# Loads of stage 3, from batch 2 on, issued by ScalarE in place of SyncE, with new due times

## The chip, the cores and the metric

The kernel runs on one core of a Trainium2 chip. The metric is the device time of one execution in microseconds, and the time of a kernel is the median of its runs. Three runs of the kernel before were timed; a fourth execution was profiled, and the rows below come from that one.

## What is computed

The input `x` has 8 batches of 2496 tokens with 256 channels. Each batch is transformed along the tokens with a real FFT, multiplied with a complex filter (one row for each of 1249 frequencies), and transformed back. The 19968 rows that come out go through a layer of 8 experts: the expert of a token is a hash of its id, and each token's row becomes `relu(row @ w1[e]) @ w2[e]` with 1024 hidden values.

```python
X = np.fft.rfft(x, axis=1)
y = np.fft.irfft(X * (filt_r + 1j * filt_i)[None], n=x.shape[1], axis=1).reshape(B * S, D)
expert_idx = token_ids * np.int64(2654435761) % np.int64(E)
for e in range(E):
    mask = expert_idx == e
    out[mask] = np.maximum(y[mask] @ w1[e], 0.0) @ w2[e]
```

## The kernel before, in words

**The filter, batch by batch.** 2496 is 39 times 64, so a transform is made in stages of small matmuls. Stage 1 (`stage1`, L581) multiplies along the 39; its result goes to a scratch tensor `d1` in DRAM (L605) and comes back with rows and columns regrouped (`load2`, L607). Stage 2 is five pieces for each batch: `forward` (L627) takes a piece to the frequencies and multiplies the filter in, `back` (L637) takes it back: TensorE makes eight matmuls, ScalarE copies the two results to SBUF (L644) and issues two DMAs of 256 KB that write them into the scratch tensor `d2` in DRAM (L646). Stage 3 (`stage3`, L662) multiplies along the 39 again; it needs the whole of `d2`, regrouped. `load4` (L648) fetches it in three parts into the tiles `t4`, of which there are two buffers: parts 0 and 1 are one DMA of 960 KB each, part 2 is two DMAs, of 480 and 160 KB. So a batch has four load4 DMAs, and the six batches from batch 2 on have 24. Each part serves two stage 3 pieces. A stage 3 piece is up to eight matmuls (L673), a copy by ScalarE (L676), two sums on VectorE (L677, L678), and four scatters by GpSimd that write each token's row to its place in the tensor `xs`, sorted by expert and stage (L708). Batches 0 and 1 are done ahead of the main loop by other functions that don't use this `load4`.

**The experts, tile by tile.** `xs` is worked off in tiles of 256 tokens, each with one expert. For each tile there is a `step(i)` (L1373); from tile 42 on it is `late_step`, with no filter work. SyncE issues the loads of the tile's two weight matrices, 1 MB each (`weights`, L739 and L742), two tiles ahead, and SyncE or ScalarE those of its rows (`load`, L1155). GpSimd makes sums of weights (`tw`, L1187). `up` (L1191) is the first product: seven products of four matmuls into three PSUM banks. ScalarE copies the first result out (`h21`, L1209). TensorE then makes products b and c, and after those the next product adds into bank a, which that copy has to have read; VectorE needs the copy as well for its sums (L1205); then come ScalarE's relus (L1202). `down` (L1228) is the second product, four blocks of eight matmuls (L1233).

**What sets the order.** Every engine works its instructions off in the order in which the program names them, and a DMA issue is an instruction of the engine that issues it. The filter's pieces are laid between the tiles by hand: `put(b, ...)` gives every piece of batch b a due time, and `run_until(t)` (L1360) emits all pieces due before t. In step i the blocks are: `run_until(i + .03)` ahead of `up`; `run_until(i + .6)` between `up` and `down`; three more inside `down`, at i + .7, .8 and .9; and `run_until(i + 1)` behind `down`, after the load of the second weight matrix. So a piece due at 18.55 is emitted between `up` and `down` of tile 18, and one due at 19.02 ahead of `up` of tile 19.

```python
run_until(i + .03)
...
up(i, ht, lambda: ask(i))
weights(i + 2, 0)
...
run_until(i + .6)
down(i, ht, lambda k: spot(i, k))
weights(i + 2, 1)
run_until(i + 1)
```

The last `back` of a batch is due at 4.48 (batch 2), 10.5, 18.5, 23.5, 31.5 and 36.5 (batch 7), so in the block between `up` and `down` of tiles 4, 10, 18, 23, 31 and 36. Before the change part 0 of load4 stands in the same block, behind it. The first stage 3 piece of each batch is due one to two tiles later (5.75, 11.85, 19.85, 24.85, 33.65, 38.65).

Of the kernel before, what the change touches and what calls it, by code (L numbers as in the profile page):

```python
# [221 lines left out]
def kernel(  # L222
# [10 lines left out]
    nc = tc.nc  # L233
# [99 lines left out]
    class Batch:  # L333
# [183 lines left out]
        def load4(self, v):  # L517
            self.t4[v] = t4pool.tile([NK, XL, C], F32, name=f"t4_{self.b}_{v}", tag="t4")
            for dram, chip in self.parts(self.d2, self.t4[v], v):
                nc.sync.dma_start(out=chip, in_=dram)  # L520
# [25 lines left out]
    class Folded(Batch):  # L546
# [101 lines left out]
        def load4(self, w):  # L648
            self.t4[w] = t4pool.tile([NK, XL, C], F32, name=f"t4_{self.b}_{w}", tag="t4")
            for dram, chip in self.moves(self.d2, self.t4[w], w):  # L650
                nc.sync.dma_start(out=chip, in_=dram)

        def room(self, u):

# [421 lines left out]
    def put(b, **at):  # L1076

        return [(t, lambda u=u, kind=kind: getattr(batches[b], kind)(u)) for kind, ts in at.items()
                for u, t in enumerate(ts) if t is not None]
# [4 lines left out]
    def row(t, n=5):  # L1084
        return [t + k for k in range(n)]
# [2 lines left out]
    todo += [(.76, lambda: [nc.sync.dma_start(out=dram, in_=chip) for dram, chip in put_off[3]])]  # L1088
    todo += [(2.3, places2)]
    todo += put(2, forward=[1.5, 1.62, 2.5, 2.62, 3.5], back=[2.48, 2.49, 3.48, 3.49, 4.48], load2=[None] * 4 + [1.63],  # L1090
                load4=[4.55, 5.1, 6.2], stage3=[5.75, 5.85, 6.65, 6.85, 7.65, 7.85])
    todo += put(3, load1=[None, None, .9], fold=[None, None, 2.8], stage1=[None] * 4 + [3.65, 3.75],
                load2=[4.1, None, 5.5, None, 7.1], forward=row(5.55), back=row(6.5), load4=[10.55, 11.3, 13.9],
                stage3=row(11.85, 6))
    todo += put(4, load1=[4.3, 6.05, 8.3], fold=[5.8, 7.8, 9.8], stage1=row(6.75, 6),
                load2=[12.05, None, 13.5, None, 15.5], forward=row(13.55), back=row(14.5), load4=[18.55, 19.3, 21.9],
                stage3=[19.85, 20.85, 21.85, 22.85, 23.65, 23.85])
    todo += put(5, load1=[10.3, 12.3, 14.1], fold=[11.8, 13.8, 15.8], stage1=[12.75, 13.75, 14.75, 15.75, 16.65, 16.75],
                load2=[17.05, None, 18.5, None, 20.5], forward=row(18.55), back=row(19.5), load4=[23.55, 24.3, 25.9],
                stage3=[24.85, 25.65, 25.85, 26.65, 26.85, 27.65])  # L1100
    todo += put(6, load1=[16.1, 17.3, 20.1], fold=[17.8, 19.8, 21.8], stage1=row(18.75, 6),
                load2=[24.05, None, 25.5, None, 28.5], forward=row(26.55), back=row(27.5), load4=[31.55, 32.3, 34.9],
                stage3=[33.65, 34.65, 35.65, 36.65, 37.65, 37.85])
    todo += put(7, load1=[22.1, 23.3, 26.1], fold=[23.8, 25.8, 27.8], stage1=row(24.75, 6),
                load2=[30.05, None, 31.5, None, 33.5], forward=row(31.55), back=row(32.5), load4=[36.7, 37.9, 39.9],
                stage3=[38.65, 38.85, 39.85, 40.85, 41.85, 42.85])
    for e, ts in enumerate(((27.05, 28, 28, 28, 29, 29.5), (28.1, 29, 29, 30, 30, 31.05), (30.05, 31, 31, 31, 32, 33.05),
                            (31.1, 32, 32, 33, 33, 34.05), (33.1, 34, 34, 34, 35, 36.05), (34.1, 35, 35, 36, 36, 37.05),
# [343 lines left out]
```

## Time and profile before

| what | value |
|---|---|
| median of three runs | 1374.3 us (1368.91 to 1377.05) |
| the profiled execution | 1381.9 us |
| its span, first to last instruction | 1380.1 us |
| mean granted TensorE clock over it | 0.991 |
| TensorE, VectorE, GpSimd, ScalarE busy | 96%, 70%, 60%, 30% of the span |
| step 0 to step 41, with the filter work of batches 2 to 7 | about 152 to 900 us |

PE is TensorE, DVE is VectorE, ACT is ScalarE, POOL is GpSimd, SP is SyncE; PEld are TensorE's weight loads. A "q" behind the name marks what an engine's sequencer does, DMA issues above all: the duration of a DMA row is that of the issue, not of the transfer. `t<-d` is a load4 DMA, `d<-mid` a write of a result into `d1` or `d2`, `mid<-d` a load2, `x<-in_x_dram` a load of input, `wts` a weight matrix, `xg<-xs` a tile's rows. In a timeline row the bracket tells how long the engine had stood idle before, and what ended that.

### The profile page before, as it was taken

Reading aid. Unit: us, or ns where it says so; the run is one execution under the profiler, and the core shown is the slowest. Engines: PE = TensorE matmul, PEld = TensorE weight load, DVE = VectorE, ACT = ScalarE, POOL = GpSimd, SP = SyncE. Lnnn points to the kernel's source line nnn. Section 1 sums busy time; section 2 is a strip of 40 time slices with the busy share of each in tenths; the row PEclk is TensorE's granted clock in tenths of the full one; section 3 lists DMA queues with packets and bytes.
Section 4 is the critical chain, followed back from the end, with each engine's and each line's share of the span. In section 5 each row is a group of like instructions: output and inputs, shape, how many; then the busy total and the mean of one; then the engine's idle time right before and its main releaser. Section 6 shows DMA issues by size and latency. Waiting matters only on the chain.

```text
span 1380.1 us, 34551 instructions
## 1 busy us (share of the span) xinstructions
PE 1329.8 (96%) x13490; PEld 1197.0 (87%) x13490; DVE 962.4 (70%) x1758; ACT 408.2 (30%) x749; POOL 826.1 (60%) x724
## 2 busy tenths in 40 slices
PE   8998999999999999989999998999999999999997
PEld 7776868788888888877888887899999999999997
DVE  6786585775576667747767786677777777777775
ACT  3546213232223222322222222122222222222222
POOL 2156526575566626748858787875665556655563
PEclk9999999999999999999999999999999999999999
DMA  8757787978787789696899878654243523271421
GB/s 229 214 187 247 172 257 190 270 216 240 189 231 234 231 233 287 174 232 198 269 308 243 249 224 241 169 178 133 63 122 102 167 76 107 48 222 41 135 49 36
DMA packets 232640, 255.74 MB, mean 185 GB/s; under 512 B 124363, under 2 KB 200896, under 8 KB 225861
## 3 DMA queue, kind: packets, MB, share of 16 engines
q1 hardware_dynamic: 124116, 163.08, 41.3%
q10 hardware_dynamic: 88357, 45.86, 13.9%
q0 software_dynamic: 20000, 44.53, 9.9%
q8 instruction: 109, 1.79, 0.6%
q14 instruction: 58, 0.48, 0.1%
HBM read 303.04 MB, written 86.15 MB: 282 GB/s over the span
## 4 chain that ended last, share of the span: by engine, by line
PE 81%; DMA 7%; DVE 5%; issue 2%; POOL 2%; ACT 1%; SPq 1%; ACTq 0%; another core or an unknown queue 0%; POOLq 0%; DVEq 0%
PE dps L1233 18%; PE up_b L1198 7%; PE up_a L1198 5%; PE dnb L1256 5%; PE upa L1256 5%; PE dna L1256 5%; PE dnc L1256 5%; PE upc L1256 5%; PE up_c L1198 4%; PE pd L673 3%; PE pa L593 3%; PE upg L1256 2%; PE upb L1256 2%; PE upe L1256 2%; PE dne L1256 2%
## 5 line engine op out<-in xcount | busy, mean ns | idle before, releaser
L1233 PE MATMUL dps<-wts,ht 128*128 128x256 f32 x1344 | 313.4, 384 | 1.1 <-ACT ht L1202 1.1
L1233 PEld LDWEIGHTS dps<-wts,ht 128*128 128x128 f32 x1344 | 252.7, 191 | 64.0 <-ACT ht L1202 24.2
L1330 POOL DMA_INDIRECT out_dram<-osb,nos x158 | 172.2, 1090 | 209.3 <-DVE osb L1271 162.6
L708 POOL DMA_INDIRECT xs<-o,sidx x176 | 181.6, 1032 | 180.0 <-DVE o L677 102.6
L1187 POOL TENSOR_TENSOR tw<-wts 128x512 f32<-128x512 f32 x158 | 203.7, 1289 | 92.8 <-DMA wts<-in_moe_w_dram 66.2
L1187 POOL TENSOR_TENSOR tw<-wts,tw 128x512 f32<-128x512 f32 x158 | 205.5, 1301 | 4.8
L1205 DVE TENSOR_TENSOR ht<-up_b,ht 128x512 f32<-128x512 f32 x126 | 87.1, 691 | 85.3 <-PE up_b L1198 59.0
L1202 ACT ACTIVATE ht<-ht 128x512 f32<-128x512 f32 x126 | 79.4, 630 | 174.3 <-DVE ht L1205 155.3
L1268 ACT ACTIVATE ht<-ht 128x512 f32<-128x512 f32 x114 | 71.7, 631 | 143.2 <-DVE ht L1271 96.4
L1198 PE MATMUL up_a<-xt,wts 128*128 128x128 f32 x672 | 95.7, 275 | 1.1 <-PE warm L1030 0.7
L1198 PEld LDWEIGHTS up_a<-xt,wts 128*128 128x128 f32 x672 | 88.3, 192 | 3.6 <-PE warm L1030 0.9
L1198 PE MATMUL up_b<-st,tw 128*128 128x128 f32 x672 | 89.3, 276 | 2.2 <-DVE ht L1205 1.4
L1205 DVE TENSOR_TENSOR ht<-up_c,ht 128x512 f32<-128x512 f32 x84 | 58.0, 691 | 41.1 <-PE up_c L1198 24.0
L1198 PEld LDWEIGHTS up_b<-st,tw 128*128 128x128 f32 x672 | 81.7, 192 | 3.0 <-issue 2.8
L1256 PE MATMUL dna<-wts,ht 128*64 128x128 f32 (+1 forms) x1152 | 79.5, 273 | 0.0
L1256 PE MATMUL upa<-filt,wts 128*64 128x128 f32 (+1 forms) x1136 | 77.5, 273 | 0.0
L1209 ACT COPY ht<-up_a 128x512 f32<-128x512 f32 x42 | 24.6, 586 | 178.0 <-PE up_a L1198 145.0
L309 DVE TENSOR_TENSOR filt<-ht 128x512 f32<-128x512 f32 x76 | 57.6, 758 | 26.6 <-ACT ht L1268 26.6
L673 PE MATMUL pd<-t,wi_t 120*117 120x256 f32 (+1 forms) x264 | 65.0, 387 | 8.1 <-DMA t<-d 8.0
L1256 PEld LDWEIGHTS dna<-wts,ht 128*64 128x64 f32 (+1 forms) x1152 | 69.4, 140 | 0.3 <-ACT ht L1268 0.2
L593 PE MATMUL pa<-x,wf_t 117*120 117x256 f32 (+1 forms) x264 | 66.1, 394 | 3.1 <-issue 1.7
L1256 PEld LDWEIGHTS upa<-filt,wts 128*64 128x64 f32 (+1 forms) x1136 | 67.6, 139 | 0.1
(231 smaller groups left out, 2541.0 us busy)
## 6 DMA issues: line engine op xcount, KB each, us to landing
wts<-in_moe_w_dram SPq DMA_DIRECT2D x162, 1024.0 KB
d_t<-t2s SPq DMA_DIRECT2D x19, 1024.0 KB
e_t<-t2s SPq DMA_DIRECT2D x19, 1024.0 KB
d<-mid ACTq DMA_DIRECT2D x60, 256.0 KB
mid<-d SPq DMA_DIRECT2D x24, 512.0 KB
x<-in_x_dram SPq DMA_DIRECT2D x39, 312.0 KB
t<-d SPq DMA_DIRECT2D x12, 960.0 KB
d<-mid ACTq DMA_DIRECT2D x11, 960.0 KB
```

The source lines that it names most:

```text
L309: eng.tensor_tensor(out_, a, b, op=op)
L593: nc.tensor.matmul(out=ps[0:cols, i - i0, :], lhsT=wf2_t[:, kind, 0:cols], rhs=self.x[w][:, i if kind == 0 else 2 * n - 1 - i, :], start=T ...
L673: nc.tensor.matmul(out=ps[kind][0:m, i, :], lhsT=wi2_t[0:r, kind, 0:m], rhs=self.t4[w][0:r, place(w, kind, 2 * half + i)[0], :], start=Tru ...
L708: st = nc.gpsimd.indirect_dma_start(out=xs[:], out_offset=bass.IndirectOffsetOnAxis(ap=index, axis=0), in_=rows, in_offset=None, bounds_ch ...
L1187: eng.tensor_tensor(t[k][:], p, q, op=OP.subtract)
L1198: nc.tensor.matmul(out=ps[bank][:, f, :], lhsT=w[:, f * P:(f + 1) * P], rhs=xx, start=first and f == 0, stop=True, skip_group_check=True)
L1202: nc.scalar.activation(out=out, in_=in_, func=AF.Relu)
L1205: nc.vector.tensor_tensor(out, ps[bank][:], other, op=OP.add)
L1233: nc.tensor.matmul(out=ps[:, h, :], lhsT=ht[:, h, fp, :], rhs=w2[:, fp, :], start=(fp == 0), stop=(fp == FP - 1))
L1256: nc.tensor.matmul(out=out[c:c + n], lhsT=w[:, c:c + n], rhs=xx, start=first, stop=True, skip_group_check=True)
L1268: nc.scalar.activation(out=out, in_=in_, func=AF.Relu)
L1330: st = nc.gpsimd.indirect_dma_start(out=out[:], out_offset=bass.IndirectOffsetOnAxis(ap=to_rows[i][:, h:h + 1], axis=0), in_=o[:, h, :], i ...
```

## The change

`load4` issues its DMAs from ScalarE's queue and no longer from SyncE's, and the due times of its parts are changed. Part 0 moves from the block between `up` and `down` to the one ahead of the next tile's `up` (in batch 2 from between to behind `down` of tile 4). Part 1 stays in its block in batches 2 to 6 (there behind the first filter piece of the next batch, where one is due in that block), and moves from behind stage 3's last piece in `down` of tile 37 to ahead of `up` of tile 38 in batch 7. Part 2 stays where it was in batch 2; in batches 3 to 7 it stands in the last block of its tile.

```diff
         def load4(self, w):
             self.t4[w] = t4pool.tile([NK, XL, C], F32, name=f"t4_{self.b}_{w}", tag="t4")
             for dram, chip in self.moves(self.d2, self.t4[w], w):
-                nc.sync.dma_start(out=chip, in_=dram)
+                nc.scalar.dma_start(out=chip, in_=dram)
...
-                load4=[4.55, 5.1, 6.2], stage3=[5.75, 5.85, 6.65, 6.85, 7.65, 7.85])
+                load4=[4.95, 5.1, 6.2], stage3=[5.75, 5.85, 6.65, 6.85, 7.65, 7.85])
...
-                load2=[4.1, None, 5.5, None, 7.1], forward=row(5.55), back=row(6.5), load4=[10.55, 11.3, 13.9],
+                load2=[4.1, None, 5.5, None, 7.1], forward=row(5.55), back=row(6.5), load4=[11.02, 11.55, 13.95],
...
-                load2=[12.05, None, 13.5, None, 15.5], forward=row(13.55), back=row(14.5), load4=[18.55, 19.3, 21.9],
+                load2=[12.05, None, 13.5, None, 15.5], forward=row(13.55), back=row(14.5), load4=[19.02, 19.55, 21.95],
...
-                load2=[17.05, None, 18.5, None, 20.5], forward=row(18.55), back=row(19.5), load4=[23.55, 24.3, 25.9],
+                load2=[17.05, None, 18.5, None, 20.5], forward=row(18.55), back=row(19.5), load4=[24.02, 24.55, 25.95],
...
-                load2=[24.05, None, 25.5, None, 28.5], forward=row(26.55), back=row(27.5), load4=[31.55, 32.3, 34.9],
+                load2=[24.05, None, 25.5, None, 28.5], forward=row(26.55), back=row(27.5), load4=[32.02, 32.55, 34.95],
...
-                load2=[30.05, None, 31.5, None, 33.5], forward=row(31.55), back=row(32.5), load4=[36.7, 37.9, 39.9],
+                load2=[30.05, None, 31.5, None, 33.5], forward=row(31.55), back=row(32.5), load4=[37.02, 38.02, 39.95],
```

## Rows read from the trace of the kernel before

**Rows 1.** The page's first part: busy time of each engine over the span.
```profile
PE 1329.8 (96%) x13490; PEld 1197.0 (87%) x13490; DVE 962.4 (70%) x1758; ACT 408.2 (30%) x749; POOL 826.1 (60%) x724
```

**Rows 2.** The waits: who waited for what, us in total, times, longest.
```profile
PE pd L673 <- DMA t<-d: 8.0, 3, 4.8
```

**Rows 3.** Timeline of PE: start, us, instruction, [idle before <- what ended it].
```profile
250.83 1.99 PE L673 MATMUL pd<-t,wi_t 120*117 120x256 f32 x8 [1.66 <-DMA t<-d]
...
604.17 3.56 PE L673 MATMUL pd<-t,wi_t 120*117 120x256 f32 x8 [4.85 <-DMA t<-d]
...
625.82 1.96 PE L673 MATMUL pd<-t,wi_t 120*117 120x256 f32 x8 [1.47 <-DMA t<-d]
```

**Rows 4.** Three stretches: busy of PE, PEld, DVE, ACT, POOL; PEclk, DMA share, GB/s.
```profile
196.00:200.00 4.00, 3.72 (x15) 2.41 (x16) 3.92 (x7) 0.00 (x0) 1.48 (x1) 0.72 0.94 293
...
600.00:604.00 4.00, 0.00 (x0) 0.00 (x0) 0.00 (x0) 0.00 (x0) 0.00 (x0) 1.00 1.13 228
604.00:608.00 4.00, 3.83 (x10) 2.98 (x11) 0.16 (x1) 0.58 (x1) 0.00 (x0) 0.58 1.07 364
```

**Rows 5.** Timeline of SyncE: load4 issues of batches 2, 3, 5 and 7.
```profile
243.24 0.36 SPq L651 DMA_DIRECT2D t<-d  x1
...
348.11 0.36 SPq L651 DMA_DIRECT2D t<-d  x1
...
581.87 6.13 SPq L561 DMA_DIRECT2D x<-in_x_dram  x3
588.11 0.90 SPq L651 DMA_DIRECT2D t<-d  x1
...
605.55 0.39 SPq L651 DMA_DIRECT2D t<-d  x1
...
860.22 8.32 SPq L651 DMA_DIRECT2D t<-d  x2
```

**Rows 6.** All load4 issues by line: duration in ns, least, median and longest.
```profile
L651 SPq DMA_DIRECT2D t<-d x24: 310/422/2029, 243.2 to 868.2; - x24
```

**Rows 7.** Timeline of ScalarE: last filter writes, next tile's copies, three instructions by them.
```profile
232.50 1.23 ACTq L646 DMA_DIRECT2D d<-mid  x2
...
239.17 0.58 ACT L1209 COPY ht<-up_a 128x512 f32<-128x512 f32 x1 [6.70 <-PE up_a L1198]
...
343.55 1.10 ACTq L646 DMA_DIRECT2D d<-mid  x2
...
349.55 0.58 ACT L1209 COPY ht<-up_a 128x512 f32<-128x512 f32 x1 [2.13 <-PE up_a L1198]
...
525.78 1.07 ACT L596 COPY mid<-pa 120x512 f32<-120x512 f32 x2 [7.58 <-DMA d<-mid]
...
584.04 0.37 ACT L676 COPY o<-pd 78x256 f32<-78x256 f32 x1 [1.74 <-PE pd L673]
...
593.79 0.85 ACTq L1155 DMA_DIRECT2D xg<-xs  x2
...
726.61 1.10 ACTq L646 DMA_DIRECT2D d<-mid  x2
...
734.14 0.58 ACT L1209 COPY ht<-up_a 128x512 f32<-128x512 f32 x1 [7.56 <-PE up_a L1198]
...
807.97 1.23 ACTq L646 DMA_DIRECT2D d<-mid  x2
...
816.36 0.58 ACT L1209 COPY ht<-up_a 128x512 f32<-128x512 f32 x1 [6.35 <-PE up_a L1198]
...
869.31 0.59 ACT L1209 COPY ht<-up_a 128x512 f32<-128x512 f32 x1
```

**Rows 8.** Timeline of PE: three places where its idle time or its order matters.
```profile
196.28 1.09 PE L623 MATMUL pb<-mid,filt 64*64 64x512 f32 x8 [2.20 <-DVE filt L633]
...
240.76 0.61 PE L1198 MATMUL up_a<-xt,wts 128*128 128x128 f32 x4
...
534.01 1.16 PE L1198 MATMUL up_c<-st,wts 128*128 128x128 f32 x8 [1.25 <-DVE ht L1205]
```

## The prediction

> **What bounds the kernel now.** I read the page's busy shares first, then the waits, then the timelines around load4. TensorE is busy for 1329.8 of 1380.1 us [rows 1], so at most some 50 us of its idle time can go at all, and a change to load4 can win only what TensorE waits for load4. The waits view gives that sum: three waits for `t<-d`, 8.0 us [rows 2]. The timeline shows them singly [rows 3]: 1.66 us ahead of batch 2's first stage 3 piece, then 4.85 and 1.47 us ahead of batch 5's first and third. The 4.85 has a second price: eight matmuls that took 1.99 us at 250.83 took 3.56 behind it, and the stretch 604 to 608 shows a granted clock of 0.58 where the one before had 1.00 [rows 3, 4]: for most of it the engine ran at 1.2 GHz in place of 2.4. That is 3.56 - 1.99 = 1.57 us more. All that load4 costs now is therefore 1.66 + 4.85 + 1.57 + 1.47 = 9.55 us. The other 21 DMAs of load4 land in time.
>
> Where the loads wait: SyncE issues them in its own order. Batch 5's part 0 was issued at 588.11, right behind three input loads that held SyncE from 581.87 to 588.00, and part 1 at 605.55 [rows 5]. The writes that part 0 needs had been issued by ScalarE in tile 23's block, one tile before.
>
> **The change, step by step.** The sum is made as differences of the profiled execution (span 1380.1 us, the execution 1381.9) and laid on the median of 1374.3, which is 7.6 us under it; I take no other difference between the two.
>
> *The issues.* 24 issues leave SyncE and come to ScalarE, at a median of 0.42 us each and 2.03 at most [rows 6]: about 10 us of ScalarE, which is busy for 408.2 us of the span [rows 1]. That costs nothing where ScalarE would stand idle, and its idle time before the next copy hides it in most places (1.74 to 7.56 us in the bracketed rows of ScalarE) [rows 7]. Where that cover is gone, as at 869.31, each DMA adds its 0.42 to the next copy.
>
> *Batch 5, parts 0 and 1.* ScalarE comes free at 584.41 (584.04 + 0.37) [rows 7], so part 0 goes out 588.11 - 584.41 = 3.7 us sooner. TensorE's wait ended 16.06 us after the issue (604.17 - 588.11) [rows 3, 5], in a stretch where the DMA engines were full (share 1.13 and 1.07) [rows 4]. If that 16 us stays, the wait shrinks from 4.85 to 1.15 us; after one of 1.66 us the clock held [rows 3], so the 1.57 go too. At best, if the load no longer stands behind the input loads, all 4.85 go; at worst the full engines only deliver in another order and nothing of this wait goes. I take 3.7 + 1.57 = 5.27, as the nearer row is the issue's own. Part 1 goes out ahead of the row loads at 593.79, some 12 us before 605.55 [rows 5, 7], for a wait of 1.47 us: all of it goes. The Trainium skill, DMA: Bandwidth & Descriptors, section "Issuing engines are not separate DMA queues", speaks against more than this: all queues share the same 16 DMA engines, so that another issuing engine saves only the time of issuing. By that rule the sum stays as I take it. The same page, section "Queues, rings and completion order", lets each DMA engine take turns between the queues that have work. By that rule the whole 4.85 would go and the sum would be 1.15 us lower; the trace of before can't decide, since no load4 of it left ScalarE's queue.
>
> *Batch 2, part 0: a new wait ahead of a copy.* The load reads what ScalarE's last two filter writes put into DRAM, so its issue waits until they have landed. In batch 2 they were issued from 232.50 to 233.73, and SyncE could issue the load only at 243.24 [rows 5, 7]. On ScalarE the load now stands ahead of tile 5's copy, which ran at 239.17 [rows 7]. The copy, and behind it the relus of tile 5 and VectorE's sums that need the copy, start at 243.24 + 0.42 = 243.66, so 4.5 us late. TensorE needs the copy's end, 239.75, only at 240.76, when it writes into bank a again [rows 7, 8]: 1.0 us of cover, and TensorE stands for 3.5 us. The 1.66 us at 250.83 vanish behind that, since the load is issued when it was. Does the clock fall? It did after 4.85 us, not after 1.66 us [rows 3, 4]; after 2.20 us at 196.28 the stretch 196 to 200 shows 0.72 [rows 4, 8]. So I charge the 1.57 again. Bounds: no stall, if the writes land as fast as in batch 3 (3.5 us after the issue: 344.65 to 348.11 [rows 5, 7]); 1 to 2 us more if the row loads and weights, which SyncE no longer holds back from 236 to 243, press on the writes. I take 3.5 + 1.57 = 5.07, the row of batch 2 itself. The Trainium skill, Perfetto Trace Analysis, section "DMA Instruction — HWDGE (DVE, Sync)", warns that the confirmation of a write can take surprisingly long where the target is HBM. The trace agrees: 3.5 us in batch 3, 9.5 in batch 2.
>
> *Part 0 of the other batches.* In batch 3 the writes had landed at 348.11; 0.42 more gives 348.5, ahead of the copy at 349.55 [rows 5, 7]: nothing. In batch 6 they were issued by 727.71 and the copy runs at 734.14, in batch 7 by 809.20 and at 816.36 [rows 7]; with the middle of 3.5 and 9.5, 6.5 us, they land at 734.2 and 815.7. I charge 0.5 us for batch 6, nothing for 7; batches 4 and 5 lie like 3 and 7.
>
> *Part 2.* Its two DMAs came back to back, but in batch 7 SyncE took 8.32 us for the pair, so an issue can wait on an older transfer as well [rows 5]. On ScalarE the pair stands ahead of the next tile's copy. At best 0.84 us inside idle time; at worst 8.3 us less the cover. Most pairs went in about the median, so I charge only batch 7, where ScalarE has no idle time ahead of 869.31 [rows 7]: 0.84 less part of the 1.0 us cover, 0.5 us.
>
> *What is freed.* SyncE's queue gives row loads and weights out sooner. TensorE waits for neither in the waits that I found, so this wins nothing; GpSimd's scatters follow stage 3 and keep their order.
>
> *The sum:* -5.27 - 1.47 - 1.66 + 5.07 + 0.5 + 0.5 = -2.3 us, so 1372.
>
> **The rivals.**
> (a) *All late loads come early.* Batch 5's first wait goes whole, and if the 7.58 us for which ScalarE stood at 525.78 hang on part 1 of batch 4, which now goes out a tile's time sooner, the 1.25 us of TensorE at 534.01 go too [rows 7, 8]. Batch 2's stall stays, without the fall of the clock: -9.55 - 1.25 + 3.5 = -7.3, 1367. For it: the input loads do stand ahead of the load. Against: the DMA engines are full where it would have to land sooner.
> (b) *ScalarE stands in the wait for its own writes in batch after batch* (slower). Mechanism: part 0 ahead of the tile's copy, while the writes land. It decides as soon as the writes take longer than the time from their issue to the copy plus 0.6 us: 7 us in batch 6, 7.7 in 7, 5.5 in 3. With batch 2's 9.5 us everywhere, the copies start at 354.57, 737.63 and 819.12, 5.0, 3.5 and 2.8 us late; less 1.0 each, 4.0, 2.5 and 1.8 us, and the clock falls in two of them: 8.3 + 3.1 = 11.4 us, in place of the 0.5 of batch 6. -2.3 + 10.9 = +8.6, 1383. For it: nothing but 10 us of DMA traffic separates batch 2 from the others. Against: batch 3's 3.5 us.
> (c) *The issue moves, the landing doesn't.* Full DMA engines deliver batch 5's load when they did; only 1.47 and 1.66 go, and the costs stay: -3.13 + 6.07 = +2.9, 1377. In batches 2 and 3 the issue can't move at all, since SyncE already issued when the writes landed.
>
> **How the numbers follow.** A measurement of this kernel can tell about 0.5%, 6.9 us, from no change. Chances: the sum 0.5, (a) 0.2, (b) 0.17, (c) 0.13. Faster by more than 0.5%: (a), just beyond that bound, and a little of the sum's spread, 0.23. Slower by more: (b) and the sum's upper bounds (part 2's waits), 0.19. The rest, 0.58, is no change. The range goes from (a) less the 5.4 us by which the lowest of the three runs lies under the median, 1362, to just beyond (b), 1384; the likeliest case alone is 1366 to 1378.
>
> **What would show each step.** Right: no wait of TensorE for `t<-d` in batch 5 and a clock of 1.00 through it; a new idle time of about 3.5 us in tile 5, ended by the copy or VectorE's sum behind it, with ScalarE waiting for `d<-mid`; no such time in the other five tiles. Wrong: the 4.85 still there (c), idle times at the start of tiles 11, 32 and 37 (b), or ScalarE long in a part 2 issue. The prediction is wrong above all if the writes' landing time differs much from the one profiled execution.

## The result, and the profile after

The kernel after takes 1389.1 us (median of four runs, 1387.8 to 1393.1), the kernel before 1373.7 us beside it (four runs, 1368.9 to 1377.1): a ratio of the means of 1.0119, with a 95% interval of 1.0082 to 1.0157. So the change makes the kernel 15.4 us slower by the medians, and the forecast of 1372 us with a range up to 1384 was wrong in sign.

The profiled execution after took 1388.4 us (span 1386.4), 0.7 us under its median. The one of before took 1381.9, 8.2 us over its median. So the two traces differ by only 6.3 us of the 15.4, and before's trace holds waits that a second trace of it doesn't have (run 4).

Page after, the busy times [rows 1], and its waits of TensorE, longest in total first (who waited for what: us in total, times, longest):

```profile
PE 1333.4 (96%) x13490; PEld 1200.3 (87%) x13490; DVE 953.9 (69%) x1758; ACT 407.8 (29%) x749; POOL 826.2 (60%) x724
```
```profile
PE up_b L1198 <- DVE ht L1205: 7.0, 8, 2.3
PE up_a L1198 <- ACT o L676: 5.0, 1, 5.0
...
PE pb L623 <- DMA mid<-d: 2.5, 2, 2.0
...
PE pd L673 <- DMA t<-d: 2.2, 2, 1.2
PE pd L673 <- issue: 2.2, 1, 2.2
```

The wait for `t<-d` went down from 8.0 us [rows 2] to 2.2, as the change would have it. Four others stand in its place. Timeline of PE after, with those four and what is left of the two in batches 2 and 5:

```profile
238.91 0.71 PE L1198 MATMUL up_a<-xt,wts 128*128 128x128 f32 x4 [1.18 <-issue]
...
248.96 1.99 PE L673 MATMUL pd<-t,wi_t 120*117 120x256 f32 x8 [1.20 <-DMA t<-d]
...
268.36 1.95 PE L673 MATMUL pd<-t,wi_t 120*117 120x256 f32 x6 [2.18 <-issue]
...
604.95 1.99 PE L673 MATMUL pd<-t,wi_t 120*117 120x256 f32 x8 [1.01 <-DMA t<-d]
...
634.85 1.22 PE L1198 MATMUL up_a<-xt,wts 128*128 128x128 f32 x4 [5.03 <-ACT o L676]
...
762.87 1.08 PE L623 MATMUL pb<-mid,filt 64*64 64x512 f32 x6 [2.02 <-DMA mid<-d]
```

Batch 5's first wait is 1.01 us where it was 4.85 [rows 3], the third piece waits no longer, and the clock holds; but at 634.85 TensorE stands for 5.03 us, and now the clock falls there. Stretches after (columns as in [rows 4]):

```profile
604.00:608.00 4.00, 3.05 (x14) 2.65 (x15) 0.92 (x2) 0.60 (x2) 0.00 (x0) 1.00 1.09 271
634.00:638.00 4.00, 2.58 (x10) 2.32 (x11) 3.05 (x5) 0.58 (x1) 3.15 (x4) 0.57 1.00 285
```

The fall has gone two tiles on: 0.57 at 634 in place of the 0.58 that before showed at 604. The eight matmuls at 604.95 take 1.99 us in place of 3.56 [rows 3]: 2.4 GHz through them.

To see where the time went, the timeline of PE was cut into tiles, each from its first `up_a` matmul to that of the next tile. Tile lengths in us; the tiles not listed, and what lies ahead of tile 0, differ by about 1.0 us at most between the first two columns. "Before again" and "after again" are runs 4 and 5 of the section below, on two chips where the kernel before takes 1358.5 and 1358.7 us:

| tiles | before | after | difference | before again | after again |
|---|---|---|---|---|---|
| 0 to 4 | 85.9 | 83.7 | -2.2 | 84.5 | 84.5 |
| 5 (batch 2, part 0) | 19.75 | 21.08 | +1.3 | 18.05 | 21.03 |
| 6 (batch 2, part 2) | 20.49 | 24.51 | +4.0 | 20.48 | 22.83 |
| 20 to 23 | 76.6 | 78.9 | +2.3 | 74.8 | 74.6 |
| 24 | 23.30 | 17.89 | -5.4 | 17.26 | 18.71 |
| 25 | 20.04 | 18.48 | -1.6 | 22.96 | 18.35 |
| 26 | 21.74 | 28.43 | +6.7 | 20.16 | 27.03 |
| 24 to 27 (batch 5) | 83.5 | 83.2 | -0.3 | 78.8 | 82.5 |
| 33 (a load2) | 16.96 | 21.73 | +4.8 | 16.96 | 16.96 |
| 36 to 43 | 129.7 | 127.4 | -2.3 | 124.3 | 128.9 |

Batch 5's gain of 7.0 us in tiles 24 and 25 comes back in tile 26. ScalarE shows how (timeline of ACT after):

```profile
588.74 0.81 ACTq L651 DMA_DIRECT2D t<-d  x1
...
633.26 0.58 ACT L676 COPY o<-pd 117x512 f32<-117x512 f32 x1 [10.68 <-DMA xs<-o,sidx]
633.29 0.88 ACTq L651 DMA_DIRECT2D t<-d  x2
634.21 0.58 ACT L1209 COPY ht<-up_a 128x512 f32<-128x512 f32 x1 [0.36 <-DMA t<-d]
```

A stage 3 copy (L676) stands for 10.68 us until a scatter has landed; part 2's pair and tile 26's copy, which TensorE needs, stand behind it. The scatter was late since GpSimd was: its first sum of tile 26's weights began at 619.95, after 9.61 us of waiting (before: 616.84, after 5.70). By the trace's clock the weights had come 3.1 us later; counted from tile 24's start they came 1.5 us sooner (29.3 against 30.8 us), but TensorE was at tile 26 7.0 us sooner. And SyncE's own waits (the DMA queue's) have a new kind, an issue of SyncE that waits for a load4 of ScalarE:

```profile
SPq L742 <- DMA t<-d: 21.5, 4, 9.4
...
SPq L613 <- DMA t<-d: 13.1, 3, 5.5
...
SPq L1155 <- DMA t<-d: 9.0, 1, 9.0
```

Before there was one such wait, of 4.0 us. L742 loads weights, L613 is load2, L1155 row loads; none of them reads `t`. Their DMAs and ScalarE's are given the same few completion semaphores (counters that tell that a DMA has landed) in turn (the trace numbers eight, 100 to 104 and 106 to 108), and an issue waits until the last DMA on its semaphore has landed. After the change tile 33's load2 is issued at 749.91, when load4's part 0, issued at 735.17 on the same semaphore, has landed at 749.90; TensorE waits 2.02 us for that load2, and the granted clock is 0.78 behind it (762 to 766 us).

### The profile page after: what moved, and what is told of

Its sections match the earlier page's. It is cut to its first block, busy times and chain, and to the rows that moved or that the text cites. A ratio compares the mean times of both kernels' runs of the same rounds, so it can differ in the third digit from the quotient of the medians.

```text
span 1386.4 us, 34554 instructions
## 1 busy us (share of the span) xinstructions
PE 1333.4 (96%) x13490; PEld 1200.3 (87%) x13490; DVE 953.9 (69%) x1758; ACT 407.8 (29%) x749; POOL 826.2 (60%) x724
## 4 chain that ended last, share of the span: by engine, by line
PE 79%; DMA 8%; DVE 4%; issue 3%; POOL 2%; SPq 1%; ACT 1%; ACTq 0%; POOLq 0%; DVEq 0%
PE dps L1233 17%; PE up_b L1198 7%; PE dnb L1256 5%; PE upc L1256 5%; PE dna L1256 5%; PE dnc L1256 5%; PE upa L1256 5%; PE up_a L1198 4%; PE up_c L1198 4%; PE pd L673 4%; PE pa L593 3%; PE upe L1256 2%; PE dne L1256 2%; PE upb L1256 2%; PE upg L1256 2%
## 5 line engine op out<-in xcount | busy, mean ns | idle before, releaser
L1209 ACT COPY ht<-up_a 128x512 f32<-128x512 f32 x42 | 24.6, 585 | 178.7 <-PE up_a L1198 145.0
```

## Experiments

All runs are on one core; those of one block ran on one chip, with the kernel before timed on it too. Ratios are against that, of the means, with their 95% interval; single times are medians. Before took 1358.5 us on the chip of runs 1 to 4, 1358.7 on that of 5 to 8, 1358.6 to 1359.3 on that of 9 to 16, and 1374.7 on that of 17 and 18, so times are never compared across chips. The first theory was that ScalarE's queue costs (A), the rivals that the due times do (B), that part 2 alone does (C), or that it is spread (D).

**1. Only the queue.** Edit: `nc.sync` to `nc.scalar` in load4, due times as before.

> Only the queue is changed: all load4 issues by ScalarE, at the old due times. Theory A (ScalarE's queue is what costs: its copies stand behind load issues, and part 0 now stands right behind the filter writes that it has to wait for): slower by at least as much as the whole change, 1389 or more, with idle times of TensorE of 2 to 5 us in the tiles behind the last back pieces (tiles 4, 10, 18, 23, 31 and 36). Theory B (the new due times cost, above all part 0 later and the loads meeting other traffic): within 0.3% of before, about 1374.

1370.5 us, ratio 1.0090 (1.0059 to 1.0121). In the waits of PE (first line below) copies held on ScalarE are the largest, four times: tiles 5, 20, 24 and 40, at 2.59, 1.88, 1.74 and 1.05 us. The size fits A, the places only in part: tiles 5 and 24 lie behind a last `back`, 20 and 40 don't, and behind those of batches 3, 4, 6 and 7 no copy is held. Tile 20 alone takes 24.24 us, 5.6 more than in before again; why isn't shown.

**2. Only the due times.** Edit: the `load4=[...]` lists of the change, issued by `nc.sync`.

> Only the due times are changed: SyncE goes on issuing. Theory A (ScalarE's queue costs): within 0.5% of before, some us slower at most, since part 0 only goes out later and the wait of 4.85 us in batch 5 grows. Theory B (the due times cost): 1385 or more.

1365.5 us, ratio 1.0061 (1.0040 to 1.0082). Neither theory: later issues on SyncE cost too, by waits for `t` (second line), 2.59 us in tile 5 and 6.30 in tile 24. Waits of PE in run 1, then in run 2:

```profile
PE up_a L1198 <- ACT ht L1209: 7.3, 4, 2.6
```
```profile
PE pd L673 <- DMA t<-d: 8.9, 2, 6.3
```

So both halves are slower alone, for different reasons, and the whole is no sum of them: tile 26 takes 19.6 us in either, so its 27 to 28 us need the new queue and the new times together.

**3. Part 2 back to SyncE.** Edit: `(nc.sync if w == 2 else nc.scalar)`, third due time of each list as before.

> Parts 0 and 1 as after the change, part 2 issued by SyncE at its old due times. Theory C (the cost sits in part 2's pairs, which stand ahead of ScalarE's copies of the next tile, in tiles 6 and 26 above all): most of the 15 us come back, 1373 to 1379. Theory D (the cost is spread, and sits in what SyncE's other loads now wait for): 1384 to 1389, as the whole change.

1366.9 us, ratio 1.0077 (1.0047 to 1.0106): C falls. But tile 6 is back at 20.49 us. Tile 26 still takes 27.06, now with no load4 ahead of its copy: TensorE stands 3.54 us for `ACT ht L1209` all the same. The pair at 633.29 is not what holds tile 26.

**4. Before again**, no edit.

> The kernel before once more, for a second profile of it. If the waits on which the prediction rests (2.20 us at 196, 1.66 us at 251, 4.85 and 1.47 us in batch 5, with falls of the clock) belong to the program, they come again within 0.5 us. If they belong to the one execution that was profiled (7.6 us over the median), some of them are smaller or gone, and the time is nearer 1374.

1355.1 us, 3.4 under the median of its chip. The 1.66 is gone and the 2.20 is 1.57. In batch 5 the two waits have changed their sizes: the 4.85 ahead of the first piece is 0.39, the 1.47 ahead of the third is 2.81. In PE's timeline:

```profile
583.60 1.99 PE L673 MATMUL pd<-t,wi_t 120*117 120x256 f32 x8 [0.39 <-DMA t<-d]
...
605.02 3.53 PE L673 MATMUL pd<-t,wi_t 120*117 120x256 f32 x8 [2.81 <-DMA t<-d]
```

The clock now falls behind the third piece's wait (3.53 us for eight matmuls) and holds behind the first's. So what load4 cost in this execution is 0.39 + 2.81 + 1.54 = 4.7 us, not 9.55, and most of it for part 1.

**5. After again**, no edit.

> The kernel after once more, on the chip of the runs beside it, as their measure. If the loss belongs to the program it is again 1.0 to 1.4% over before. In its profile the long steps should come again: tile 5 some 2.5 us longer than its 18.05 us without an idle time, tile 6 with TensorE held by ScalarE's late copies, tile 26 by the copy that stands behind a scatter, tile 33 by a late load2. Those that don't come again were of one execution.

1368.3 us, ratio 1.0073 (1.0046 to 1.0099). Tiles 5, 6 and 26 come again, tile 33 doesn't. From here on they are the places to be explained.

**6. Batch 5 alone; 7. all but batch 5.** Edits: `(nc.scalar if self.b == 5 else nc.sync)` with batch 5's new times, and the reverse.

> Only batch 5's three parts go to ScalarE with their new due times. Theory E (the 16 DMA engines are full from part 0 to the scatters of tile 26, so what load4 wins the weights, and GpSimd's sums and scatters behind them, lose): within 0.2% of before, with no wait for t in tile 24 over 1.5 us, and steps 24 to 27 together within 1.5 us of those of before. The prediction's step (5.27 + 1.47 us won): ratio 0.995. A loss of 3 us or more: batch 5 is one of the places that make the change slow.

> Everything of the change but batch 5, which stays with SyncE at its old times. Theory E (batch 5 neither wins nor costs): as much over before as the whole change, 1.0 to 1.4%. Prediction's step: 0.5% worse than the whole change. If batch 5 costs: better than the whole change by 3 us or more.

Batch 5 alone: 1.0015 (0.9992 to 1.0038); tile 24 waits 0.82 us for `t`, tiles 24 to 27 take 80.8 us, 2.0 more than in before again, where E allowed 1.5; by the medians it is 3.2 us slower. All else: 1.0040 (1.0017 to 1.0063), tile 6 at 22.82. So batch 5 wins nothing, and over half of the loss is elsewhere. The prediction's step for batch 5 falls.

**8. Part 0 back to SyncE.** Edit: `(nc.sync if w == 0 else nc.scalar)`, first due time of each list as before.

> Part 0 of each batch stays with SyncE at its old time, parts 1 and 2 go to ScalarE. Theory F (part 0 costs: it stands ahead of ScalarE's copy while the filter writes land, tile 5, and in batch 6 it now gets in ahead of load2, tile 33): half of the loss or more goes, ratio 1.006 or less, with tile 33 back at 16.96 us. Theory G (the cost sits in parts 1 and 2 as much): 1.008 or more.

1.0071 (1.0044 to 1.0098): F falls as the main cause. Tile 5 is back at 18.02 us, so part 0 does cost there, but tile 6 takes 24.60 and tile 26 27.28.

**9. Batch 2's part 2 alone.** Edit: `(nc.scalar if self.b == 2 and w == 2 else nc.sync)`, times as before.

> Only batch 2's part 2 (two DMAs) goes to ScalarE, at its old place. Read from the profile's tile 6 alone. Theory G (the pair of issues holds ScalarE's two copies behind it, the next filter piece finds no free PSUM, and TensorE stands 2.2 us): tile 6 takes 22.8 us or more, in place of the 20.49 that every kernel with part 2 at SyncE showed. If tile 6's 2.3 us came from part 0 or 1 instead: 20.5 us.

Tile 6 takes 22.83 us: shown. How is another matter than expected. Timelines of PE and DVE, first in this run, then in before again:

```profile
258.01 0.67 DVE L633 TENSOR_TENSOR filt<-pb,filt 128x512 f32<-128x512 f32 x1
...
258.78 1.96 PE L673 MATMUL pd<-t,wi_t 120*117 120x256 f32 x8 [2.18 <-issue]
```
```profile
257.90 1.89 PE L673 MATMUL pd<-t,wi_t 120*117 120x256 f32 x8
...
259.46 0.68 DVE L633 TENSOR_TENSOR filt<-pb,filt 128x512 f32<-128x512 f32 x1
```

With SyncE's issue the stage 3 piece starts 1.56 us before VectorE reads `pb`; with ScalarE's it starts as that reading ends (258.01 + 0.67 = 258.68). The same in after: 268.36, behind an L633 that ends at 268.25. ScalarE's copies were held for only 0.38 us. In all eight traces that have this pair at ScalarE the piece starts 0.10 us after such a reading has ended; in the twelve others it starts 10.05 us after tile 6's first `up_a`, with no wait. TensorE's instructions are the same and in the same order, but in the trace's wait fields the wait of the first four matmuls for ScalarE is gone, and that of the second four stays. So `pd` seems to have got another buffer in PSUM, TensorE's output memory: one which VectorE must read out first, and no longer one that ScalarE had emptied. No wait field names VectorE; that the buffer changed when the program was built is read from these waits and times and wasn't tried apart.

**10. Batch 5 with a later part 1; 11. after, with sooner scatters; 12. batch 5 with sooner scatters.**

```diff
 10: load4 engine: (nc.scalar if self.b == 5 and w < 2 else nc.sync)
-                load4=[23.55, 24.3, 25.9],
+                load4=[24.02, 24.75, 25.9],
 11: in the kernel after; 12: in the kernel of run 6
-            now = len(parts_) if self.b == 2 and u > 3 else 2
+            now = len(parts_) if (self.b == 2 and u > 3) or (self.b == 5 and u == 0) else 2
```

> Batch 5 alone: part 0 goes to ScalarE with its new time, part 1 to ScalarE too, but inside the second product of tile 24, so after the weights of tile 26 have been issued; part 2 stays with SyncE. Theory H (part 1, issued beside those weights, takes their share of the DMA engines; they land some 7 us later, and with them GpSimd's sums and scatters, which hold a buffer that ScalarE's copy in tile 26 needs): the weights take under 16 us in place of 20.9 and 23.1, tile 26 takes 19.6 to 21 us, and the ratio is 0.995 to 1.000. Theory I (tile 26 is held because ScalarE has the issue, whenever): tile 26 takes 26 us or more, ratio 1.001 or more.

> As after the change, but GpSimd writes batch 5's first stage 3 piece with all four scatters at once, and does not keep two of them until it has the weights of tile 26. Theory H: the buffer is free in time, tile 26 takes 19.6 to 21 us in place of 27.0 to 28.4, and some 6 to 7 us of the change's loss go: ratio 1.001 to 1.004. If the buffer were not what holds ScalarE's copy: tile 26 takes 26 us or more, ratio 1.006 or more.

> Batch 5's loads at ScalarE with their new times, all else as before, and the four scatters at once. Theory H, and with it the prediction's step that batch 5's loads are won by the earlier issue: tiles 24 to 27 take 74 to 76 us in place of 78.8 to 83.5, and the ratio is 0.995 to 0.998, faster than before. If what is won there is always lost in the same stretch to the full DMA engines: 79 us or more and a ratio of 1.000 to 1.002.

Theory H rests on the chain in tile 26. Issue of one weight matrix by SP and GpSimd's first sum of it, in before again and in after again:

```profile
580.77 2.57 SPq L739 DMA_DIRECT2D wts<-in_moe_w_dram  x1
...
595.74 1.36 POOL L1187 TENSOR_TENSOR tw<-wts 128x512 f32<-128x512 f32 x1 [6.75 <-DMA wts<-in_moe_w_dram]
```
```profile
580.10 4.14 SPq L739 DMA_DIRECT2D wts<-in_moe_w_dram  x1
...
603.37 1.27 POOL L1187 TENSOR_TENSOR tw<-wts 128x512 f32<-128x512 f32 x1 [9.07 <-DMA wts<-in_moe_w_dram]
...
615.94 0.59 ACT L676 COPY o<-pd 117x512 f32<-117x512 f32 x1 [9.53 <-DMA xs<-o,sidx]
...
617.58 1.22 PE L1198 MATMUL up_a<-xt,wts 128*128 128x128 f32 x4 [3.93 <-ACT ht L1209]
```

Measured from tile 24's first `up_a` (569.9 and 573.8), the matrix is asked for after 10.9 us in the one and 6.3 us in the other, so sooner, and used after 25.8 and 29.6 us, so later: 15.0 against 23.3 us from issue to use. In the first, part 1 goes out 4.4 us behind it on SyncE's own queue (585.13), in the second 0.8 us behind it on ScalarE's (580.93). Two scatters of the stage 3 piece stand behind these sums in GpSimd's order, the copy behind the scatters, TensorE behind the copy. All traces go the same way: from issue to use this matrix takes 14.5 to 17.4 us in the eight with batch 5's loads at SyncE and their old times (before, 4, 7, 9, 13, 14, 16 and 17), and 18.8 to 26.0 us in the ten with part 0 or 1 at ScalarE at a new time (after, 3, 5, 6, 8, 10, 11, 12, 15 and 18).

Run 11: 1.0028 (1.0011 to 1.0045), against 1.0073 of after again; the intervals just miss each other. 10.68 and 9.53 us of the copy become 2.01, a wait for TensorE itself:

```profile
611.13 0.59 ACT L676 COPY o<-pd 117x512 f32<-117x512 f32 x1 [2.01 <-PE pd L673]
```

So the buffer held by late scatters is what stopped ScalarE in tile 26: shown. The tile is shorter, but by 2.6 us, not 6: 24.38. TensorE now stands 1.85 us for weights in tile 25 and 2.55 us for a later copy in tile 26.

Run 10: 0.9980 (0.9958 to 1.0001), as H expected, but its profile shows tile 26 at 27.77 us and weights as late as in after again. That execution took 1365.1 us, the longest of twelve with a median of 1356.8, so it can't speak for them. But the weights took 24.4 us in it, and 18.8 and 19.9 in runs 15 and 18, with the same due time of part 1: the "under 16 us" came in none. That a later part 1 spares the weights is not shown.

Run 12: 0.9987 (0.9968 to 1.0006). Tiles 24 to 27 take 79.1 us, not 74 to 76: tile 26 is shorter (21.71), but tile 27 takes 21.69 in place of 18.43. This half of the expectation fell. What bounds these tiles together isn't shown.

**13. and 14. Two more MB.** Edit, at 23.97 and at 21.97:

```diff
+    extra = nc.dram_tensor("extra", (2, F, C), F32)
...
+    todo += [(23.97, lambda: [nc.sync.dma_start(out=extra[k], in_=moe_w2[k]) for k in range(2)])]
```

> As before the change, with two DMAs of 1 MB each more (weights copied to a spare tensor that nobody reads), issued by SyncE at the end of tile 23's block, so into batch 5's stretch. Theory E (DMA engines full in tiles 24 and 25): tiles 24 to 27 take 5 to 8 us more than the 78.8 to 83.5 without (2 MB at some 250 to 300 GB/s), ratio 1.004 to 1.006. If the stretch is bound by something else: within 2 us, ratio 1.001 or less.

> The same two DMAs issued two tiles earlier, at the end of tile 21's block, into a stretch with a DMA share of 0.67. Theory E: they are hidden in the idle third of the engines, tiles 22 and 23 take no more than 1 us more, ratio 1.000 to 1.002. If any 2 MB cost, wherever they are: as the run beside it.

Run 13: 1.0050 (1.0021 to 1.0079), and tiles 24 to 27 take 85.6 us, 6.7 over before again, as theory E expected. Nearly all of it is in one wait, 2.81 us in before again:

```profile
609.72 3.73 PE L674 MATMUL pd<-t,wi_t 120*117 120x256 f32 x8 [9.10 <-DMA t<-d]
```

This is the wait for part 1, which SyncE issues behind the two. It issued them in 5.82 us (1.22 in run 14), part 1 goes out 3.7 us later against tile 24 than in before again and is used 6.2 us later. So the run doesn't tell the full DMA engines from SyncE's own queue.

Run 14, meant as the harmless case, cost 1.0037 (1.0010 to 1.0065). Tiles 20 to 23 are not longer (73.9 us), as expected: the 2 MB themselves are hidden. But tile 24 takes 24.80 us. SyncE's waits and timeline, with ScalarE's and PE's rows (lines are one or two higher than in the other kernels, so L562 is the input load L561):

```profile
SPq L562 <- DMA d<-mid: 15.1, 1, 15.1
```
```profile
547.72 0.10 SPq L740 DMA_DIRECT2D wts<-in_moe_w_dram  x1
...
559.25 1.10 ACTq L647 DMA_DIRECT2D d<-mid  x2
...
562.93 2.79 SPq L562 DMA_DIRECT2D x<-in_x_dram  x3
...
577.67 2.05 PE L1200 MATMUL up_b<-st,tw 128*128 128x128 f32 x8 [5.65 <-DVE ht L1207]
```

An input load that was issued at 539.14 in before again waits here until 562.93, for a filter write that ScalarE issues only at 559.25 and that has nothing to do with it but the semaphore (both 106). VectorE then stands for the input, and TensorE 5.65 us behind VectorE. Two DMAs more had shifted which of the eight semaphores each later DMA gets. This is the crossed wait by itself: shown.

**15. Later part 1 and sooner scatters together; 16. before with sooner scatters.** Edits: those of 10 and 11 on the kernel before; that of 11 alone.

> Batch 5's parts 0 and 1 at ScalarE, part 1 inside the second product of tile 24, part 2 at SyncE as before, and the four scatters of batch 5's first stage 3 piece at once. If both remedies add up (0.2% and 0.3% less were measured for them apart): ratio 0.994 to 0.997, the best of all. If the DMA engines bound the stretch: 0.997 to 1.000, as each alone.

> The kernel before with the four scatters at once, all loads at SyncE. Theory H (scatters kept behind the weights hold the buffer): the hold of ScalarE's copy in tile 26 goes here too, but TensorE hardly stood for it (tile 26 took 20.2 us): ratio 0.998 to 1.000. If the gain in the kernel with batch 5 at ScalarE (0.9987) came from the scatters alone: the same 0.9987.

Run 15: 0.9984 (0.9962 to 1.0005), tile 26 at 19.57, tiles 24 to 27 at 78.5 us: no more than each alone, as E has it; TensorE waits 2.76 us for part 1. Run 16: 1.0018 (0.9991 to 1.0044), over what either theory expected, though its interval reaches H's range. Its trace, of the fastest of its twelve runs (1352.9 us), has the shortest tiles 24 to 27 of all, 75.9 us, with every load at SyncE. The DMA share is 1.06 and 1.08 in its tiles 24 and 25, as full as elsewhere. So that the full DMA engines set the length of this stretch isn't shown. The remedies of batch 5 give nothing that can be told from before; 10, 12 and 15 agree in sign, and none of them is a version that surely beats it.

**17. Batch 2 alone; 18. the change with both places mended.**

```diff
 17: (nc.scalar if self.b == 2 else nc.sync), batch 2's new times
 18: in the kernel after, with run 11's edit:
-                nc.scalar.dma_start(out=chip, in_=dram)
+                (nc.sync if self.b == 2 or (self.b == 5 and w == 2) else nc.scalar).dma_start(out=chip, in_=dram)
...
-                load4=[4.95, 5.1, 6.2],
+                load4=[4.55, 5.1, 6.2],
...
-                load4=[24.02, 24.55, 25.95],
+                load4=[24.02, 24.75, 25.9],
```

> Only batch 2's three parts go to ScalarE, with their new times. If tile 5's held copy (2 to 3 us) and tile 6's pair of issues (2.35 us) are the loss of the change outside batch 5 (1.0040): tile 5 takes 20.5 to 21.2 us, tile 6 22.8 or more, ratio 1.003 to 1.004. If batches 3, 4, 6 and 7 carry it: 1.001 or less.

> The change with both places mended: batch 2 stays with SyncE at its old times, batch 5's part 1 goes out inside the second product of tile 24 and its part 2 by SyncE, and batch 5's first four scatters go at once; batches 3, 4, 6 and 7 as after. If the two places carry the loss: ratio 0.997 to 1.001, as the kernel with batch 5 alone so mended (0.9984). If the other four batches cost as well: 1.003 or more.

Run 17: 1.0026 (1.0004 to 1.0047), tile 5 at 20.50 and tile 6 at 24.52 us; the medians lie further apart, 1381.5 against 1374.7. Run 18: 0.9998 (0.9981 to 1.0015). With batches 2 and 5 mended the loss is gone, and batches 3, 4, 6 and 7 on ScalarE cost nothing that can be measured.

## Why the prediction was wrong

**Batch 5, part 0 (-5.27) and part 1 (-1.47).** This step failed, and the first two traces hide half of it. In them the load goes out 4.0 us sooner against its tile (2.1 us behind tile 24's first `up_a` before, 1.9 ahead of it after), the wait ends 16.2 us after the issue as it did in 16.06, 1.01 us of it are left (1.15 forecast), the clock holds, and part 1's wait is gone. For part 0 this agreement is luck. With SyncE at the old time the wait for it ended 13.6 to 13.8 us behind tile 24's first `up_a` in runs 4, 7, 9 and 13, and took 0.2 to 0.5 us; in 8 and 16 there was none. With ScalarE at the new time the load goes out 2.6 to 2.8 us sooner against the tile, and the wait ended after 13.5 to 15.2 us (runs 3, 5, 6, 10, 11, 12 and 15) and took 0.1 to 1.8 us. On the slower chip it ended after 15.4 us in run 17 (SyncE) and 15.5 in run 18 (ScalarE). The issue of part 0 and TensorE's first piece, in before again and in after again (tile 24 begins at 569.89 and 573.75):

```profile
570.80 0.61 SPq L651 DMA_DIRECT2D t<-d  x1
...
583.60 1.99 PE L673 MATMUL pd<-t,wi_t 120*117 120x256 f32 x8 [0.39 <-DMA t<-d]
```
```profile
571.88 1.50 ACTq L651 DMA_DIRECT2D t<-d  x1
...
588.91 1.99 PE L673 MATMUL pd<-t,wi_t 120*117 120x256 f32 x8 [1.83 <-DMA t<-d]
```

So "if that 16 us stays" failed: from issue to the wait's end it is 12.7 to 13.0 us in those runs with SyncE and 15.3 to 17.0 in those with ScalarE. The issue moved, the landing hardly did, and there was hardly a wait to win. Issued 5.1 us ahead of the tile, as in run 1, it isn't waited for at all. Part 1 was worth more than forecast: 2.1 to 3.3 us in runs 4, 7, 9 and 16, and 0.2 us or less with part 1 at ScalarE in every run but 15.

The other half is that the step ended at the wait: where a stall goes, something else is late next. The DMA engines are full in this stretch, as the prediction itself said [rows 4]; tile 26's weights take longer beside the earlier loads, scatters and a copy stand behind them, and TensorE stands in tile 26 instead. Tiles 24 to 27 together won 0.3 us in the two first traces, not 6.74; on the faster chips they take 80.8 to 82.5 us with the loads at ScalarE and the new times (runs 3, 5 and 6) against 78.5 to 79.5 at SyncE with the old ones (4, 7 and 9), and batch 5 alone gave 1.0015. The Trainium skill, DMA: Bandwidth & Descriptors, section "Issuing engines are not separate DMA queues", says that the DMAs of every issuing engine run on the same 16 DMA engines, and that issuing from several saves only the time of issuing. The traces agree: issued sooner and from ScalarE, part 0 is waited for until 13.5 to 15.2 us, against 13.6 to 13.8. The prediction weighed this only as a limit on the load's own gain and didn't ask what is delivered later for it. The Trainium skill, DMA: Bandwidth & Descriptors, section "Queues, rings and completion order", has each DMA engine take turns between the queues. That didn't take the whole 4.85 away: 1.01 us is left.

**Part 2 ("I charge only batch 7").** The mis-placed term. Batch 7's pair showed no cost in the trace of after; batch 2's, charged with nothing, costs 2.35 us (22.83 - 20.48), or 4.0 to 4.1 where the granted clock falls as well (0.66 in after's 270 to 274 us), in every trace that has it and in none that hasn't (after, 1, 5, 7, 8, 9, 11 and 17 against before, 2 to 4, 6, 10, 12 to 16 and 18). The idle time ahead of ScalarE's copies was counted, the buffers behind them were not.

**Batch 2, part 0 (+5.07 - 1.66 = +3.4).** Right in kind: a copy held, 1.18 us of TensorE, no fall of the clock, and the load goes out as the writes land (237.90; they had been issued by 230.55). Too large by some 1.5: tile 5 took 20.5 to 21.2 us in the six profiles with this load at ScalarE and its new time (after, 3, 5, 7, 11 and 17), and 18.0 to 19.8 in eleven of the twelve with it at SyncE and its old time (21.7 in run 6): about 1.9 us apart. The 1.66 us that were to vanish behind it stayed as 1.20 in the trace of after.

**The price of load4 before (9.55).** One execution, 8.2 us over its median. Before again showed 4.7. The waits for batch 5's loads, 6.32 us in the trace that was used, are 2.1 to 4.7 us in the five others of the old order (4, 7, 9, 16 and 17), and in the four of them on the faster chips nearly all for part 1.

**What is freed ("wins nothing").** It lost something: SyncE's DMAs come to wait for ScalarE's by the shared semaphores. Tile 33's +4.8 us is of this kind, in the first trace of after; it was 0 in after again and in run 18 and 1.6 to 2.1 in runs 3, 7 and 11. In all five of those the load2 goes out 0.01 to 0.02 us after load4's part 0 has landed, so the crossing is the program's, but whether TensorE then waits is not. How much of the 15.4 us it is in the median stays open.

**The rivals.** (b) had the sign but not the mechanism: tiles 11, 32 and 37 are as long as before within 0.2 us. (a) fell. (c) was right for part 0 of batch 5, whose landing didn't move with its issue on the faster chips; its sum of 1377 still lacked tile 26's hold and batch 2's part 2. The sum of what was found, from the runs: batch 2 1.0026 (on the slower chip), batch 5 1.0015, the whole 1.0073 on a faster one. The rest of 0.3% is within these intervals, and crossed waits may be in it; on the first chip the whole was 1.0119, and that difference wasn't tried.

## What to carry to other kernels

A wait for a transfer in a stretch where the DMA engines are full may not be won by issuing that transfer sooner: here it landed no sooner, or something else landed later. Sum the stretch, and name what lands later. A moved DMA moves more than itself: the order in which completion semaphores and buffers are handed out shifts for what comes behind it, so list after a move which unrelated issues now wait for whom. And profile the kernel before twice before a gain of a few us is worked out from one trace's waits.

## What was not expected of the hardware

Two DMAs of 1 MB that nobody reads, hidden in a stretch with a DMA share of 0.67 (533 to 551 us of run 4), held an unrelated input load for 15.1 us by a shared completion semaphore (run 14). A weight matrix of 1 MB took 15.0 us from issue to use beside one load4 order and 23.3 beside another (runs 4 and 5). And chips differ: the kernel before took 1358.5 us on one and 1374.7 on another, a ratio of 1.012, as large as the effect studied; tiles 7 to 19 alone took 226.8 and, in the trace of before shown first, 231.1 us.
